# Six triangular inverses by two 16-step blocks and a join on TensorE, GpSimd's products moved to VectorE, softmax scalars to ScalarE

## The chip, the cores and the metric

One core of a Trainium2 chip. The metric is device time in microseconds, the median of several executions of one program. Engines are named as in the profile: PE (TensorE), DVE (VectorE), ACT (ScalarE), POOL (GpSimd), SP (SyncE, which only issues DMAs here).

## What is computed

A linear recurrence over 768 steps for 32 heads with 40x40 states, then two feed-forward blocks on its 3072 x 320 output (cut to what matters):

```
for t in range(S):
    y[t] = r[t] @ state
    Sa = state @ a[t]
    state = state * w[t] - outer(Sa, b[t]) + outer(v[t], k[t])
x = y                                    # 3072 x 320
h = x @ w_in                             # 320 -> 1024
solu = h * softmax(h)
x = ((solu - mean) / sqrt(var + 1e-6) * g) @ w_out
h = x @ w2_in                            # 320 -> 2048
out = (max(h, 0) + alpha * min(h, 0)) @ w2_out
```

The weights of both blocks arrive as 64-bit floats; the kernel rebuilds 32-bit values from their words ("decodes" them) and splits each into a high and a low part.

## The kernel before

**Stages.** The start (0 to 41 us) prepares windows 0 and 1. Then 24 slots (41 to 775 us): slot g takes 32 steps of the recurrence for all heads. In a slot PE runs, in this order, px (L654), pu (L669), pf (L694), pst (L708), pg (L747), pss (L728) and py (L772); each result passes through ACT or DVE before the next stage may use it. From slot 3 on the first feed-forward block is woven in as a queue of pieces (h L815, ptr L874, po L890 to L892, ptx L906), three slots behind. After the slots the second block runs nearly alone on PE (ph L1367, acc L1385 to L1387), with a short tail of the first.

**The order.** PE, DVE, ACT and POOL run the order in which the program is written out. `slot` writes it with a model of time: `now` is PE's clock in the plan, `run(e, cost, f, ...)` writes an instruction for engine e and advances e's planned time by a cost in microseconds. Work that is not urgent lies in the lists `work["dec"]`, `["inv"]`, `["scan"]`, `["xs"]`, from which `fill` takes the first that is ready. Where the plan has PE wait, and also where too few columns were streamed lately, `pop` writes a filler matmul ("busy" L315 in slots 0 to 3, "zero" L275 later); `flush(n)` writes the queued feed-forward pieces until n are left. SP's queue takes the DMAs in the order of writing.

**What the change touches.**
- The inverse of a 32x32 unit triangular matrix for every group of four slots (NT, read by pu and pf). `first_inverse` (group 0) splits it in two 16x16 blocks: 14 steps of a multiply and an add on DVE (L563, L566), a product with a mask (L571), a transpose (L573), and then two sets of small matmuls, pv and pn (L579). `inverse` (groups 1 to 5) does all 31 steps on DVE (L503, L507, L531) between two 128x1024 transposes (L515, L534).
- Each window (two slots) clamps the decay factors into a copy wc (L372), runs four scans over it (L376, L380) and multiplies kbf by the result on DVE (L430) and XS on POOL (L442).
- The masked pg of a slot: ACT copies PSUM to YS (L758), POOL multiplies by the mask (L752), py reads it.
- The low part of Y: POOL (L789). Then `x_move` writes Y to DRAM and reads it back transposed (L799 to L801).
- Softmax: four one-column operations on DVE (L822, L823, L834, L838).
- Decoding: four DVE operations per chunk (L932, L933, L940, L944), two on ACT, one product on POOL (L952); the raw words come by L969. `ND`, `NC`, `NL` say how many chunks of the second block's weights are due in each slot: the first four slots, the middle ones, the last four.

Of the kernel before, what the change touches and what calls it, by code (L numbers as in the profile page):

```python
# [45 lines left out]
def tile_kernel(ctx: ExitStack, tc: tile.TileContext, w_fm, a0_fm, a_fm, kb_fm, r_fm, v_fm, v_tm,  # L46
# [25 lines left out]
    half = flp.tile([128, 1], F32, name="half")  # L72
    xd = [dr.tile([640, 256], F32, name=f"xd{w}") for w in range(NW)]
# [62 lines left out]
    def init():  # L136
# [19 lines left out]
        nc.gpsimd.memset(half, -0.5)  # L156
        nc.gpsimd.memset(one, 1.0)
# [194 lines left out]
    def scan_steps(w, pe):  # L352
# [3 lines left out]
        def first():  # L356
# [47 lines left out]
    def prep_window(w):  # L404
# [32 lines left out]
    def mult_a(g, e, *pes):  # L437
# [4 lines left out]
        (nc.vector if w < 2 and e in DA else nc.gpsimd).tensor_tensor(out=o, in0=o, in1=h, op=ALU.mult)  # L442
# [5 lines left out]
    def gen1(g, half):  # L448
# [42 lines left out]
    def inverse(W):  # L491
        M, NT = LMN[2 * W % 3], LMN[(2 * W + 1) % 3]
        N = NT.rearrange("p s t -> p t s")

        P = PR[W > 0]

        def rank1(eng, tmp, s, rows):
            nt = 31 - s
            l = N[:, s + 1:32, s]
            tv = tmp[:, 0:sum(b - a for a, b in rows) * nt].rearrange("p (i t) -> p i t", t=nt)  # L500
            for a, b in rows:
                sh = [128, b - a, nt]
                eng.tensor_tensor(out=tv[:, a - rows[0][0]:b - rows[0][0]], in0=M[:, a:b, s:s + 1].to_broadcast(sh),  # L503
                                  in1=l.unsqueeze(1).to_broadcast(sh), op=ALU.mult)
            for a, b in rows:
                o = M[:, a:b, s + 1:32]
                r = eng.tensor_tensor(out=o, in0=o, in1=tv[:, a - rows[0][0]:b - rows[0][0]], op=ALU.add)  # L507
            return r

        def pool_rows():  # L510
            for s in range(P, 31):
                rank1(nc.gpsimd, b1.tile([128, TM], F32, name="tmp2", tag="Yt"), s, [(P, s + 1)])

        def start():
            nc.vector.transpose(out=N, in_=st["lraw", W].rearrange("p l t -> p t l"))  # L515
            run("P", 1.2, lambda: unit(M, nc.gpsimd), free["V"])
            pool_rows()

        def step(s):
            n, nt = min(s + 1, P), 31 - s  # L520
            m = n // 2
            if n <= SM:
                ops = [(M[:, i, s + 1:32], N[:, s + 1:32, s], M[:, i, s:s + 1]) for i in range(n)]
            elif nt <= SM:
                ops = [(M[:, 0:n, s + 1 + i], M[:, 0:n, s], N[:, s + 1 + i, s:s + 1]) for i in range(nt)]
            else:
                rank1(nc.vector, b1.tile([128, 256], F32, name="tmp"), s,
                                   [(0, m), (m, n)] if W == 0 else [(0, n)])
                return
            for o, x, f in ops:  # L530
# [1202 lines left out]
```

## Time and profile before

| what | us |
|---|---|
| median of 3 runs (1165.24 to 1170.81) | 1168.54 |
| the profiled execution | 1164.45 |
| its span | 1162.7 |
| start, 0 to 41.2 | 41.2 |
| slots 0 to 3, 41.2 to 197.2 | 156.0 |
| slots 4 to 19, 197.2 to 676.3 | 479.1 |
| slots 20 to 23, 676.3 to 774.7 | 98.4 |
| second block, 774.7 to 1162.7 | 388.0 |
| PE / DVE / ACT / POOL busy in the span | 1026.6 / 770.2 / 532.6 / 498.2 |

The bounds of a slot are the starts of its copy of px (XP, L657). [...]

### The profile page before, as it was taken

The numbers are of one execution on the slowest core, as the hardware profiler recorded it, in microseconds if no ns is written. First come the engines' busy times: TensorE is split into PE (matmuls) and PEld (weight loads), VectorE is DVE, ScalarE is ACT, GpSimd is POOL, SyncE is SP. The second block draws the span as 40 slices with busy tenths as digits, with TensorE's granted clock in tenths as the row PEclk, the third lists the DMA queues.
The fourth block names the chain that finished last, engine by engine and source line by source line (L and its number), as shares of the span: only waits on it lengthen the run. The fifth ranks groups of instructions, "written<-read, shape, count | busy, mean of one in ns | idle before, by whom it ended". The sixth has DMA issues, their size and how long they took to land. (4 is left out here: it accounts for less than half of the span.)

```text
span 1162.7 us, 38709 instructions
## 1 busy us (share of the span) xinstructions
PE 1026.6 (88%) x16801; PEld 818.1 (70%) x16801; DVE 770.2 (66%) x1471; ACT 532.6 (46%) x1218; POOL 498.2 (43%) x509
## 2 busy tenths in 40 slices
PE   6789686787868988888889989999899999999997
PEld 3455363676645766676657767779799999999996
DVE  8777898886869869778987974257434334443343
ACT  1355452564634754756447656658712121212121
POOL 6448556363325534553344323436233333333332
PEclk8789888888989989998999999999999999999999
DMA  5625542244332542443324532345502020201010
GB/s 167 156 72 136 139 136 70 71 125 107 97 102 81 134 131 59 129 128 105 81 57 124 155 83 62 79 130 185 174 1 66 4 65 4 66 4 45 1 24 14
DMA packets 106740, 103.70 MB, mean 89 GB/s; under 512 B 38340, under 2 KB 85188, under 8 KB 106564
## 3 DMA queue, kind: packets, MB, share of 16 engines
q1 hardware_dynamic: 106564, 101.17, 31.7%
q8 instruction: 133, 2.18, 0.8%
q14 instruction: 43, 0.35, 0.1%
HBM read 75.71 MB, written 25.43 MB: 87 GB/s over the span
## 5 line engine op out<-in xcount | busy, mean ns | idle before, releaser
L1374 POOL TENSOR_TENSOR gll<-gt,gh 128x512 fp32r<-128x512 f32 (+1 forms) x112 | 129.3, 1155 | 227.1 <-ACT gh L1373 224.4
L850 DVE TENSOR_SCALAR gt<-ph,al 128x512 f32<-128x512 f32 (+1 forms) x112 | 75.4, 674 | 189.0 <-PE ph L1367 188.9
L1373 ACT CAST gh<-gt 128x512 fp32r<-128x512 f32 (+1 forms) x112 | 62.6, 559 | 253.3 <-DVE gt L851 218.4
L752 POOL TENSOR_TENSOR YS<-YS,mask 64x512 f32<-64x512 f32 x48 | 64.9, 1353 | 105.3 <-ACT YS L758 103.4
L815 PE MATMUL h<-w1h,xt 128*128 128x512 f32 x240 | 91.2, 436 | 16.9 <-ACT h L836 16.9
L1386 PE MATMUL acc<-w2l,gh 128*128 128x320 f32 x288 | 89.0, 309 | 0.0
L1387 PE MATMUL acc<-w2h,gll 128*128 128x320 f32 x288 | 88.9, 309 | 0.0
L1385 PE MATMUL acc<-w2h,gh 128*128 128x320 f32 x288 | 88.9, 309 | 0.0
L890 PE MATMUL po<-wo1h,lnh 128*128 128x320 f32 x192 | 66.9, 348 | 21.6 <-DVE lnl L880 19.6
L442 POOL TENSOR_TENSOR XS<-XS,H 40x512 f32<-40x512 f32 (+1 forms) x48 | 70.0, 1461 | 35.2 <-DVE H L376 23.0
L952 POOL TENSOR_TENSOR dec<-em 128x256 f32<-128x256 f32 x44 | 38.0, 864 | 107.4 <-DVE em L944 58.9
L315 PE MATMUL busy<-busy 128*128 128x512 bf16 x292 | 80.1, 426 | 4.3 <-DVE busy L1281 3.0
L275 PE MATMUL zero<-D 104*128 104x512 bf16 x299 | 76.5, 393 | 1.5 <-DVE XS L482 1.5
L851 DVE SCALAR_TENSOR_TENSOR gt<-ph,gt 128x512 f32<-128x512 f32 (+1 forms) x112 | 68.8, 615 | 3.8
L507 DVE TENSOR_TENSOR LMN<-LMN,tmp 128x87 f32<-128x87 f32 (+8 forms) x135 | 67.7, 502 | 4.6
L503 DVE TENSOR_TENSOR tmp<-LMN,LMN 128x87 f32<-128x87 f32 (+8 forms) x135 | 67.6, 501 | 2.8
L892 PE MATMUL po<-wo1h,lnl 128*128 128x320 f32 x192 | 62.0, 323 | 4.4 <-DVE lnl L880 4.4
L815 PEld LDWEIGHTS h<-w1h,xt 128*128 128x128 f32 x240 | 44.7, 197 | 27.4 <-ACT h L836 20.6
L815 PE MATMUL h<-w1l,xt 128*128 128x512 f32 x144 | 62.7, 435 | 0.0
L622 ACT COPY KBS<-pt 64x160 f32<-64x160 f32 x192 | 55.1, 287 | 16.7 <-PE pt L618 14.4
L891 PE MATMUL po<-wo1l,lnh 128*128 128x320 f32 x192 | 61.7, 321 | 0.0
L1367 PE MATMUL ph<-w1h,w2h 128*128 128x512 f32 x180 | 59.4, 395 | 0.0
(209 smaller groups left out, 2705.6 us busy)
## 6 DMA issues: line engine op xcount, KB each, us to landing
kbf<-in_kb_fm_dram SPq DMA_DIRECT2D x24, 416.0 KB
x2d<-x SPq DMA_DIRECT2D x24, 320.0 KB
raw<-in_w_in_dram SPq DMA_DIRECT2D x24, 256.0 KB
xd<-Y SPq DMA_DIRECT2D x24, 256.0 KB
xt<-xd SPq DMA_DIRECT2D x12, 512.0 KB
raw<-in_w_out_dram SPq DMA_DIRECT2D x20, 256.0 KB
wt<-in_w_fm_dram SPq DMA_DIRECT2D x24, 211.7 KB
VUS<-in_v_tm_dram SPq DMA_DIRECT2D x48, 80.0 KB
```

Of the source, the lines that this page charges most:

```text
L275: nc.tensor.matmul(st["z"][0], lhsT=D1[:, 1:65].bitcast(BF16), rhs=D1[:, 0:256].bitcast(BF16), start=True, stop=True)
L315: nc.tensor.matmul(st["busy"], lhsT=busy[:, 0:128], rhs=busy, start=True, stop=True)
L442: (nc.vector if w < 2 and e in DA else nc.gpsimd).tensor_tensor(out=o, in0=o, in1=h, op=ALU.mult)
L503: eng.tensor_tensor(out=tv[:, a - rows[0][0]:b - rows[0][0]], in0=M[:, a:b, s:s + 1].to_broadcast(sh), in1=l.unsqueeze(1).to_broadcast(sh) ...
L507: r = eng.tensor_tensor(out=o, in0=o, in1=tv[:, a - rows[0][0]:b - rows[0][0]], op=ALU.add)
L815: nc.tensor.matmul(st["h"][:, ns], lhsT=l, rhs=r, start=j == 0, stop=j == len(ops) - 1)
L850: nc.vector.tensor_scalar(out=tmp, in0=h, scalar1=0.0, scalar2=al, op0=ALU.min, op1=ALU.mult)
L851: nc.vector.scalar_tensor_tensor(out=o, in0=h, scalar=0.0, in1=tmp, op0=ALU.max, op1=ALU.add)
L1374: nc.gpsimd.tensor_tensor(out=gll, in0=t, in1=f32(gh), op=ALU.subtract)
L1385: nc.tensor.matmul(acc, lhsT=gh[:, cs], rhs=oh, start=f == 0, stop=False)
L1386: nc.tensor.matmul(acc, lhsT=gh[:, cs], rhs=ol, start=False, stop=False)
L1387: nc.tensor.matmul(acc, lhsT=gll[:, cs], rhs=oh, start=False, stop=f == K2 - 1)
```

## The change

All six inverses use the two blocks and the join; GpSimd's products on XS, YS, Y and the first block's weights go to VectorE (the masked pg now straight from PSUM, so ACT's copy goes); the clamp of the decay factors goes, and the scans read wt; the softmax's small operations become three on ACT; the second block's decoding starts at slot 4; up to 10 feed-forward pieces stay queued before py (RES) and 8 at the end of a slot (KQ); and costs given as a tuple occupy, in the plan, a "port" that VectorE and GpSimd use one at a time.

```
-VS, NC, NL = 0, (2, 3, 1, 0), (3, 3, 3, 0)
-ND = (6, 6, 4, 2)
-RES = 2
-PR, SM, TM = (10, 32), 2, 121
+VS, NC, NL = 0, (2, 3, 3, 3), (3, 3, 3, 0)
+ND = (0, 0, 0, 0)
+KQ, RES = 8, 10
+YSV, XSV, YLV, DPV, VRV, W1V = 1, 1, 1, 0, 0, 1
...
         if not plain():
-            free[e] = max(free[e], *needs) + cost
+            t = max(free[e], *needs)
+            if isinstance(cost, tuple):
+                cost, = cost
+                for a, b in sorted(port):
+                    if a < t + cost and b > t:
+                        t = b
+                port.append((t, t + cost))
+                del port[:-6]
+            free[e] = t + cost
...
-            for s in ORDER[e]:
+            for s in ("dec",) * (st["slot"] % 4 < 3) + ORDER[e]:
...
-            nc.vector.tensor_scalar(out=wz[:, :, 1:65], in0=wv, scalar1=W_MAX, scalar2=W_MIN, op0=ALU.min, op1=ALU.max)
-            nc.vector.memset(wc[:, ::65], 0.0)
...
-        (nc.vector if w < 2 and e in DA else nc.gpsimd).tensor_tensor(out=o, in0=o, in1=h, op=ALU.mult)
+        (nc.vector if XSV or w < 2 and e in DA else nc.gpsimd).tensor_tensor(out=o, in0=o, in1=h, op=ALU.mult)
...
     def inverse(W):
-        M, NT = LMN[2 * W % 3], LMN[(2 * W + 1) % 3]
...
-    def first_inverse():
-        X, F = LMN[0], LMN[1]
+        X, F, A = LMN[(W + 1) % 2 if W else 0], LMN[(W + 1) % 2], LMN[2]
...
+        vec = [(2.2, start)] + [((0.38 + s * (15 - s) / 240.0,), lambda s=s: step(s)) for s in range(1, 15)] + [(2.0, fin)]
+        return vec, (0.75, low), [lambda: (left(0), left(1)), lambda: (join(0), join(1))]
...
+            for pe in range(2):
+                t = run("V", 0.43, lambda e=e, q=q, pe=pe: nc.vector.tensor_tensor(
+                    out=y[q, e, pe * 8:pe * 8 + 8], in0=pg[64 * pe:64 * pe + 64, :, e],
+                    in1=mask[64 * pe:64 * pe + 64].unsqueeze(1).to_broadcast([64, 8, 32]), op=ALU.mult), now[0] + PL)
...
-                        ("P", 1.3, lambda: nc.gpsimd.tensor_tensor(out=l, in0=Yt, in1=f32(h), op=ALU.subtract))], end)
+                        ("V" if YLV else "P", (0.7 if YLV else 1.3,), lambda: (nc.vector if YLV else nc.gpsimd).tensor_tensor(out=l, in0=Yt, in1=f32(h), op=ALU.subtract))], end)
...
         def small():
-            nc.vector.tensor_scalar(out=col(5), in0=col(1), scalar1=1e-9, scalar2=None, op0=ALU.add)
-            nc.vector.tensor_scalar(out=col(6), in0=col(5), scalar1=col(5), scalar2=1e-6, op0=ALU.mult, op1=ALU.mult)
+            nc.scalar.activation(out=col(6), in_=col(1), func=AF.Square, scale=1e-3, bias=tiny)
+            nc.scalar.activation(out=col(7), in_=col(4), func=AF.Identity, scale=1.0 / F1, bias=col(6))
...
-        for tasks in (turns, gens):
+        for tasks in (joins, turns, gens):
...
+            inverted(W + 1, p(2, 'z'), p(3, 'z'))
...
-        if g == 1:
+        if g == 2:
             until(lambda: decoded(6))
         stage_y(g)
         side(g, "z")
-        flush(0)
+        flush(0 if fin else KQ)
```

What moves on the engines, at three places. First PE in slot 8, the first that needs group 2's inverse (po is a feed-forward product, zero a filler, pu the first reader of the inverse, LMN). Before, 28 fillers stand directly in front of pu, 73 in the slot:

```order
L891 MATMUL po<-wo1l,lnh 128x320
L892 MATMUL po<-wo1h,lnl 128x320
L275 LDWEIGHTS D_148
L275 MATMUL zero<-D_148 128x512
...
L669 MATMUL pu<-XP,LMN_166 32x40 x12
```

and now:

```order
L593 MATMUL px<-VUS_168,XS_153 32x40 x32
L842 MATMUL po<-wo1h,lnh 128x320
L843 MATMUL po<-wo1l,lnh 128x320
L844 MATMUL po<-wo1h,lnl 128x320
...
L608 MATMUL pu<-XP,LMN_166 32x40 x32
L620 LDWEIGHTS D_149
L620 MATMUL pf<-D_149 32x256
L633 MATMUL pf<-LMN_166,XP 40x32 x16
```

No filler stands in slot 8 any more: three feed-forward pieces left over from the slot before stand in front of pu. Counted over the whole order by the same slot bounds, the fillers go from 232 to 174 in slots 0 to 3, from 239 to 127 in slots 4 to 19 and from 60 to 15 in slots 20 to 23.

Second, DVE in slot 9 up to the product that follows py (Yt). Before:

```order
L430 TENSOR_TENSOR kbf<-kbf,F 104x16x32
L713 TENSOR_TENSOR VUS_167<-pst,VUS_168 40x320 x4
L880 TENSOR_TENSOR lnl<-ptr,lnh 128x512 x2
L932 TENSOR_SCALAR em_5789<-raw_5739 128x256
...
L829 TENSOR_REDUCE sm<-h 128x1
...
L776 TENSOR_TENSOR Yt<-py,H 104x512
L834 TENSOR_SCALAR sm<-sm 128x1
```

and now:

```order
L443 TENSOR_TENSOR XS_153<-XS_153,H 40x512 x2
L443 TENSOR_TENSOR XS_154<-XS_154,H 40x512
L652 TENSOR_TENSOR VUS_168<-pst,VUS_169 40x320 x2
...
L431 TENSOR_TENSOR kbf<-kbf,F 104x16x32
...
L697 TENSOR_TENSOR YS_173<-pg_5872,mask 64x256 x4
L884 TENSOR_SCALAR em_5919<-raw_5863 128x256
...
L722 TENSOR_TENSOR Yt<-py,H 104x512
L785 TENSOR_REDUCE sm<-h 128x1
L736 TENSOR_TENSOR Y<-Yt,Y 104x16x32
```

XS, YS and Y's low part, which were POOL's, stand in DVE's row of work, and the one-column sm operation is gone.

Third, SP where window 4's Y moves through DRAM (xd and xt). Before:

```order
L799 DMA xd_72<-Y 32x8x256
L799 DMA xd_72<-Y 8x8x256
L800 DMA xt<-xd_72 128x4x256
...
L801 DMA xt<-xd_72 128x256
L349 DMA XS_154<-in_a_fm_dram 40x512
L969 DMA raw_6128<-in_w_out_dram 128x512
```

and now:

```order
L751 DMA xd_73<-Y 32x8x256
L751 DMA xd_73<-Y 8x8x256
L752 DMA xt<-xd_73 128x4x256
L923 DMA raw_6211<-in_w_in_dram 128x512
L753 DMA xt<-xd_73 128x256
```

The raw words of a decode chunk stand close behind xt, which waits for xd, in both.

## Rows read from the trace of the kernel before

**Rows 1.** Busy time by stage: us; PE, PEld, DVE, ACT, POOL; clock; DMA
```profile
197.20:676.30 479.10, 406.23 (x9412) 312.95 (x9412) 394.39 (x811) 276.91 (x673) 205.59 (x230) 0.92 0.39 105
774.70:1162.70 388.00, 375.11 (x2201) 342.42 (x2199) 164.83 (x263) 113.17 (x210) 139.44 (x121) 0.99 0.18 55
```
**Rows 2.** The same view of the fillers alone: "busy", then "zero" twice
```profile
41.20:197.20 156.00, 62.22 (x232) 21.87 (x232) 0.06 (x1) 0.00 (x0) 0.87 0.43 114
...
197.20:676.30 479.10, 59.24 (x228) 0.92 0.39 105
676.30:774.70 98.40, 13.16 (x53) 1.00 0.30 76
```
**Rows 3.** Groups of DVE in the slots, the five 31-step inverses
```profile
L507 DVE TENSOR_TENSOR LMN<-LMN,tmp 128x87 f32<-128x87 f32 (+8 forms) x135 | 67.7, 502 | 4.6
L503 DVE TENSOR_TENSOR tmp<-LMN,LMN 128x87 f32<-128x87 f32 (+8 forms) x135 | 67.6, 501 | 2.8
...
L515 DVE STREAM_TRANSPOSE LMN<-LMN 128x1024 f32<-128x1024 f32 x5 | 10.6, 2127 | 0.0
```
**Rows 4.** The same view of the one two-block inverse (group 0)
```profile
L566 DVE TENSOR_TENSOR LMN<-LMN,tmp 128x28 f32<-128x28 f32 (+6 forms) x14 | 3.4, 244 | 0.4
L563 DVE TENSOR_TENSOR tmp<-LMN 128x28 f32<-128x28 f32 (+6 forms) x14 | 3.4, 242 | 0.4
...
L573 DVE STREAM_TRANSPOSE VT<-V 128x512 f32<-128x512 f32 x1 | 1.1, 1093 | 0.0
```
**Rows 5.** Groups of PE in the slots: group 0's join, its two sets
```profile
L579 PE MATMUL pn<-VR,LMN 32*32 32x32 f32 x256 | 3.6, 213 | 2.3 <-issue 2.1 <-ACT LMN L589 0.2
L579 PE MATMUL pv<-VT,GR 16*32 16x16 f32 x256 | 2.7, 180 | 1.6 <-DVE VT L573 1.2 <-issue 0.4
```
**Rows 6.** Other groups of DVE in the slots
```profile
L482 DVE TENSOR_TENSOR XS<-pg,mask 32x256 f32<-32x256 f32 x80 | 33.2, 415 | 2.9 <-ACT LMN L473 1.9
...
L932 DVE TENSOR_SCALAR em<-raw 128x256 int32<-128x256 int32 x44 | 18.7, 426 | 37.9 <-DMA raw<-in_w_out_dram 20.8 <-DMA raw<-in_w_in_dram 13.5 <-POOL dec L952 3.3
...
L372 DVE TENSOR_SCALAR wc<-wt 104x512 f32<-104x512 f32 x19 | 12.2, 641 | 13.3 <-DMA wt<-in_w_fm_dram 13.2
...
L838 DVE TENSOR_SCALAR sm<-sm 128x1 f32<-128x1 f32 x21 | 4.4, 208 | 7.3 <-ACT h L836 6.5
```
**Rows 7.** Line L430 by itself: shortest/median/longest ns, first and last start
```profile
L430 DVE TENSOR_TENSOR kbf<-kbf,F x44: 674/690/1777, 12.0 to 625.1; 104x512 f32<-104x512 f32 x44
```
**Rows 8.** DVE in order of time (start, duration), slot 8
```profile
355.73 3.86 DVE L430 TENSOR_TENSOR kbf<-kbf,F 104x512 f32<-104x512 f32 x3
...
361.27 1.68 DVE L430 TENSOR_TENSOR kbf<-kbf,F 104x512 f32<-104x512 f32 x1
```
**Rows 9.** POOL in order of time, the same stretch
```profile
355.86 6.54 POOL L442 TENSOR_TENSOR XS<-XS,H 40x512 f32<-40x512 f32 x4
```
**Rows 10.** Groups of POOL in the slots
```profile
L752 POOL TENSOR_TENSOR YS<-YS,mask 64x512 f32<-64x512 f32 x48 | 64.9, 1353 | 105.3 <-ACT YS L758 103.4
L442 POOL TENSOR_TENSOR XS<-XS,H 40x512 f32<-40x512 f32 x40 | 59.6, 1489 | 25.9 <-DVE H L376 15.0 <-issue 7.8 <-DMA XS<-in_a_fm_dram 1.0
```
**Rows 11.** Who DVE waited for in slots 4 to 19: us, times, longest
```profile
DVE em L932 <- DMA raw<-in_w_out_dram: 20.1, 4, 9.4
DVE wc L372 <- DMA wt<-in_w_fm_dram: 13.2, 3, 7.0
```
**Rows 12.** Who PE waited for in the same stretch
```profile
PE po L890 <- DVE lnl L880: 19.0, 4, 9.6
PE h L815 <- ACT h L836: 14.3, 4, 12.7
```
**Rows 13.** SP in order of time, slot 8
```profile
329.57 0.39 SPq L800 DMA_DIRECT2D xt<-xd  x1
330.06 0.45 SPq L969 DMA_DIRECT2D raw<-in_w_out_dram  x1
```
**Rows 14.** DVE in order of time, slot 8
```profile
334.74 0.29 DVE L932 TENSOR_SCALAR em<-raw 128x256 int32<-128x256 int32 x1 [9.45 <-DMA raw<-in_w_out_dram]
```
**Rows 15.** Busy time by stage again: slots 9 and 10
```profile
379.00:402.40 23.40, 21.97 (x634) 17.22 (x632) 19.61 (x38) 18.09 (x47) 13.93 (x15) 1.00 0.52 144
402.40:432.90 30.50, 25.54 (x525) 20.47 (x526) 20.98 (x47) 15.70 (x39) 9.59 (x14) 0.83 0.43 116
```

More of the change, by code (lines that the diff above doesn't have):

```diff
@@ L491, in inverse @@
     def inverse(W):
-        M, NT = LMN[2 * W % 3], LMN[(2 * W + 1) % 3]
[L493 to L530, printed above, removed]
-                nc.vector.scalar_tensor_tensor(out=o, in0=x, scalar=f, in1=o, op0=ALU.mult, op1=ALU.add)
@@ L590, in left @@
                 ring[bk] = t + LAT
[L591 removed]
+                put(("left", W))(t + LAT)
         def join(h):
             ls = range(16 * h, 16 * h + 16)
[L595 removed]
+            until(("left", W))
             p, bk = bank([128, 16, 32], "pn")
@@ L599, in join @@
             ring[bk] = t + LAT
-            st["NT", 0] = F
-            put(("NT", 0))(t + LAT)
-        yield start
-        for s in range(1, 15):
-            yield lambda s=s: step(s)
-        yield fin
-        for f in (left, join):
-            for h in range(2):
-                yield lambda f=f, h=h: f(h)
+            st["NT", W] = F
+            put(("NT", W))(t + LAT)
+        vec = [(2.2, start)] + [((0.38 + s * (15 - s) / 240.0,), lambda s=s: step(s)) for s in range(1, 15)] + [(2.0, fin)]
+        return vec, (0.75, low), [lambda: (left(0), left(1)), lambda: (join(0), join(1))]
     def trans(w, q):
@@ L860, in soft @@
             return
-        chain(now[0] + PL, s[:5], lambda u: (put("h")(u), chain(
-            u, s[5:] + [("A", 1.27, lambda: norm(P, m))], put(("P", t)))))
+        chain(now[0] + PL, s[:4], lambda u: (put("h")(u), chain(
+            u, s[4:] + [("A", 1.27, lambda: norm(P, m))], put(("P", t)))))
     def tr1(t, j):
@@ L991, in rest, with zero @@
                 def rest():
-                    nc.gpsimd.tensor_tensor(out=w1l[:, k, cs], in0=o, in1=f32(w1h[:, k, cs]), op=ALU.subtract)
+                    (nc.vector if W1V else nc.gpsimd).tensor_tensor(out=w1l[:, k, cs], in0=o, in1=f32(w1h[:, k, cs]), op=ALU.subtract)
+                    if k == 2 and not W1V:
+                        zero()
+                def zero():
                     if k == 2:
@@ L997, in steps @@
                     ("A", 0.63, lambda: nc.scalar.copy(out=w1h[:, k, cs], in_=o)),
-                    ("P", 2.6 if k == 2 else 1.4, rest)]
+                    ("B", ("dec", (0.7,)), rest) if W1V else ("P", (2.6 if k == 2 else 1.4,), rest)] + [
+                        ("P", 1.2, zero)][:W1V * (k == 2)]
             return steps
@@ L1044, in ended @@
             q["done"] += 1
+            if q["wide"] and q["done"] == 6 and "moved" in st:
+                moved()
             if not q["wide"]:
@@ L1143, in slot_tasks, with inverted @@
             load_a(2 * u + 1)
-            lr = [("lr", h) for h in range(4 * W + 4, 4 * W + 8)]
-            inv = list(inverse(W + 1))
-            for i, (cost, f) in enumerate(inv):
-                work["inv"].append((lambda: max(map(at, lr)), cost, f,
-                                    put(("NT", W + 1)) if i == len(inv) - 1 else None))
+            inverted(W + 1, p(2, 'z'), p(3, 'z'))
         if c4 >= 2 and w < NW:
             load_a(2 * w + c4 - 2)
+    def inverted(W, first, last):
+        lr = [("lr", h) for h in range(4 * W, 4 * W + 4)]
+        vec, (cost, low), (lj, rj) = inverse(W)
+        for i, (c, f) in enumerate(vec):
+            work["inv"].append((lambda: max(map(at, lr)), c, f, None if i < len(vec) - 1 else
+                                lambda t: chain(t + LAT, [("A", cost, low)], lambda u: put(("VT", W))(u))))
+        joins.append((first, last, lambda: at(("VT", W)), lj))
+        joins.append((first, last, lambda: at(("left", W)), rj))
     def mlp_tasks(g):
@@ L1274, in phase1 @@
             kb_load(2)
-        inv = list(first_inverse())
-        st["joins"] = inv[16:]
-        for i, f in enumerate(inv[:16]):
+        vec, (_, low), st["joins"] = inverse(0)
+        for i, (_, f) in enumerate(vec):
             f()
```

104 lines of the change are left out of this document (46 added, 58 removed).

## The prediction

> **What bounds the kernel now.** I read the busy time by stage first. In the second block PE is busy 375.1 of 388.0 us [rows 1]; the change leaves that stage's instructions alone but for four softmaxes in its tail, so nothing is to be had there. The slots are another matter. In slots 4 to 19 DVE works 394.4 of 479.1 us and PE's own figure holds 59.2 us of "zero" fillers [rows 1, 2], which are written where the plan has PE wait or stream too little. [...]
>
> [...] (1) The inverse: groups 1 to 5 put 67.7 + 67.6 us of multiply and add and ten long transposes on DVE [rows 3], and slot 8 carries 73 fillers in front of and around its reader. (2) The exclusion between DVE and POOL: four kbf products in slot 8 take 3.86 + 1.68 us, though a product of that form alone takes 0.69 (the median; 0.67 the shortest, 1.78 the longest), and POOL's four XS products run in the very same stretch, 6.54 us [rows 7 to 9]. Each waits for the other. The masks that read PSUM show no such spread worth a term: their mean is 0.415 us [rows 6]. (3) A DMA: DVE stands 9.45 us in slot 8 until raw words land; their load was issued at 330.06, behind xt at 329.57, which had to wait for xd [rows 13, 14]. Such waits sum to 20.1 us for the one kind of raw words and 13.2 us for wt [rows 11], and PE's longest waits in this stretch, 19.0 us for lnl of DVE and 14.3 us for h of ACT [rows 12], are partly behind them.
>
> **The change part by part: slots 4 to 19.** On DVE, in us over the 16 slots:
> - Inverse. Five take 67.7 + 67.6 and two kinds of transposes at 10.6 each, so (156.5)/5 = 31.3 apiece [rows 3]. The two-block form takes 3.4 + 3.4, three transposes at 1.09 and one 128x512 product, for which I take kbf's 0.69: 10.8 [rows 4, 7]. Four of the five fall here: 4 x 20.5 = -82.
> - The clamp wc: 12.2/19 = 0.64 per half window, one per slot: -10 [rows 6].
> - Softmax: four one-column operations, of at most 0.21 each [rows 6], say 0.7 together: -11. They become three on ACT, which is busy 276.9 of 479.1 us [rows 1]; at 0.21 each that is 10 us, covered by its idle time. If it were not, the chain of a softmax would be that much later, 0.6 us per slot.
> - Masks from PSUM: four per slot at 0.415 (nearest row: the same kind of product, L482): +27. ACT loses its copies and POOL 64.9 us in all slots [rows 10].
> - XS: two per slot, two inputs in SBUF, 512 elements, like kbf: 0.69 (bounds 0.67 and 1.78): +22. Y's low part, the same form, +11.
> - Decoding: 18 chunks that ND placed in slots 0 to 3 now fall here, four operations of about 0.43 each [rows 6]: +31.
> - Exclusion: XS and YS leave POOL, two of its dearest readers (59.6 and 64.9 us [rows 10]). In slot 8 the four kbf products lost 5.54 - 4 x 0.69 = 2.8 us; eight windows at most 22, and none at least, since the median over all 44 did not wait. I take -16, with the smaller losses of the other forms.
>
> Sum: -28, so DVE's busy time goes from 394 to some 366 of these slots. What of that reaches the clock depends on DVE's idle 85 us. If all of it stays, the slots shrink by 28; if the shown DMA waits (33 us) vanish too, by 61. The order speaks against the second: the raw load stands close behind xt in the new program as well. For some of it speaks that 8 to 10 feed-forward pieces may now be carried past a slot's end, so PE has work when a late operand blocks it. From PE's side: 239 - 127 = 112 fillers at 59.24/228 = 0.26 are 29 us less, the two waits for lnl and h (33 us) perhaps halved, 17; against it four more joins at 3.6 + 2.7 = 6.3 us [rows 5], +25, and some clock won back. That gives -21 and a little more. I take the middle of DVE's two ends: **-45**, ends 0 and -80 (below).
>
> **Slots 0 to 3.** 232 fillers become 174: 58 x 62.22/232 [rows 2] = **-16**. What makes the room is 18 chunks fewer (31 us of DVE) and a shorter inverse against masks, XS, Y and 22 products of the first block's weights (22 x 0.69 = 15). One join more (6 us) stands in slot 3, where fillers stood. Ends 0 and -30: DVE is nearly always busy there, so a decode chunk in the wrong place costs its whole length.
>
> **Slots 20 to 23.** 60 fillers become 15; the trace has 53 in these bounds, 13.16 us, 0.25 each [rows 2]: 38 x 0.25 = **-9**. The last inverse, which slot 20 waited for, is the reason.
>
> **The rest.** The start loses five clamps of DVE, less than 0.7 us each, of which at most one is on the path to the first matmuls: 0 to -1, taken as 0. SP issues the same DMAs. In the tail, PE's 375 of 388 us cover the softmax [rows 1]; without that cover it would be 4 x 0.7.
>
> Sum: 1164.45 - 45 - 16 - 9 = 1094. The runs' median stands 4.1 us above this execution, well inside what I cannot know, so I leave **1094 us**. Differences within 0.5% (6 us) are what a measurement of this kernel can't tell from none.
>
> **The rivals.**
> (a) *Everything shown as a wait was made by the inverse and the exclusion, and goes.* Then slots 4 to 19 run like slot 9, 23.4 us, plus a quarter of a join, 1.6: 16 x 25 = 400, -79, and 1060 in all. For it: slot 9 had DVE at 19.6 of 23.4 us [rows 15], and the average after is 366/16 = 22.9. Against: the raw load still queued behind xt. 20%.
> (b) *The gain on DVE is eaten by PE's joins and by what is moved.* DVE's 28 us shrink the slots, 25 us of joins find no gap, and nothing else falls: slots 4 to 19 at about -3, 1136 in all. For it: work goes from POOL, busy 205.6 of 479.1 us, to the engine that is the fullest [rows 1]. [...] 14%.
> (c) *The clock falls with the fillers.* If every one of the 16 slots ran like slot 10 instead of six of them, 3.6 us more PE time each [rows 15], ten slots would lose 36 and the 45 would shrink to 9: 1130 to 1148. Against: the slots at the lower clock are those with DMA waits, not those without fillers; slot 9 has none in the order and runs at 1.00. [...] 5%.
> (d) *Slower: the masks queue.* DVE takes its work in order. YS, XS and Y now stand in a row with scans and kbf products; py waits for the mask, and if two long operations (1.7 us each, as the slow kbf [rows 8]) stand ahead of it at one point of each slot with no piece for PE, that is 3.4 x 24 = 82 us, and 1176. It decides from 70/24 = 2.9 us per slot. Against: in the new order the masks stand next to decode operations of 0.4 us, and PE has pieces in stock. 6%.
> (e) *No change*, several of these together: 3%.
>
> **How the numbers follow.** The forecast (1075 to 1115) has 52%, (a) 20%, (b) 14%, (c) 5%, (d) 6%, (e) 3%. The range 1047 to 1140 leaves out a part of (a) and of (b), half of (c), and (d) and (e), some 2 in 10. Faster by over 0.5%: forecast, (a), (b), (c), 91%; same 3%; slower 6%.
>
> **What would show it.** DVE's busy time in slots 4 to 19 near 366 us; kbf's products all near 0.69; two-block inverses at 10.8 us of DVE each; about 127 zero fillers and no long wait in slots 8 and 16; waits of DVE for raw words still there, 20 to 40 us; second block within 2 us of 388. The prediction is wrong if slots 4 to 19 take under 400 or over 460 us; then the row to look at is DVE's idle time, and who ended it.

## The result and the profile after

The changed kernel takes **1135.78 us** (median of 4 runs, 1133.65 to 1136.73) against 1166.89 us for the kernel before on the same chip: a ratio of 0.9734 (95% interval 0.969 to 0.9778), 31 us faster. The forecast was 1094 us, a gain of 70 on the execution it started from. The direction was right, the size less than half. The profiled execution took 1136.73 us, its span is 1134.9. By stage (bounds of a slot as before):

| stage | before, us | after, us | change | forecast |
|---|---|---|---|---|
| start | 41.2 | 41.0 | -0.2 | 0 |
| slots 0 to 3 | 156.0 | 140.0 | -16.0 | -16 |
| slots 4 to 19 | 479.1 | 478.6 | -0.5 | -45 |
| slots 20 to 23 | 98.4 | 83.8 | -14.6 | -9 |
| second block | 388.0 | 391.5 | +3.5 | 0 |

Nearly all that is missing is missing in slots 4 to 19. The busy time by stage, columns as in [rows 1]: stretch, its length, PE, PEld, DVE, ACT, POOL, clock, DMA share, GB/s:

```profile
41.00:181.00 140.00, 117.72 (x3307) 74.69 (x3308) 102.50 (x224) 57.58 (x135) 13.18 (x23) 0.84 0.37 101
181.00:659.60 478.60, 418.10 (x11342) 335.56 (x11340) 349.27 (x745) 279.67 (x688) 93.96 (x146) 0.89 0.42 113
659.60:743.40 83.80, 81.41 (x1881) 67.03 (x1881) 45.81 (x93) 59.58 (x140) 19.52 (x26) 0.98 0.35 93
743.40:1134.90 391.50, 378.52 (x2222) 347.86 (x2222) 164.40 (x254) 115.93 (x222) 140.37 (x123) 0.99 0.19 55
```

The same view of the filler "zero" alone (stretch, length, PE, clock, DMA share, GB/s):

```profile
181.00:659.60 478.60, 33.52 (x127) 0.89 0.42 113
```

Against [rows 1, 2], DVE's work in slots 4 to 19 fell from 394.39 to 349.27 us, even more than forecast, and its idle time grew from 85 to 129 us: the engine was relieved and the slots did not get shorter. PE tells why. Its busy time rose by 11.9 us although fillers fell by 25.7, so its other work rose by 37.6; its idle time fell by only 12.4. 37.6 - 25.7 - 12.4 = -0.5, the whole change of the stretch. Of the 37.6 us, 25.9 are the small matmuls of the four joins that now stand here (pv and pn, below); the rest is other work that took longer.

Who PE waited for in slots 4 to 19 (total, times, longest). "issue" stands where PE waited for nothing that the profile shows:

```profile
PE pn L523 <- issue: 10.6, 5, 4.1
PE pv L523 <- issue: 5.9, 4, 2.0
PE pg L686 <- ACT VUF L636: 4.9, 1, 4.9
...
PE pu L608 <- issue: 2.8, 1, 2.8
PE po L843 <- issue: 2.5, 1, 2.5
PE pss L667 <- issue: 2.5, 2, 2.2
```

The long waits of [rows 12] for lnl and h are gone (the longest for h is 1.3 us). In their place "issue" takes 29.7 us in nine rows; before, two rows of pg had 1.0 us each. pv and pn are the two sets of small matmuls of a join. Their groups in all slots:

```profile
L523 PE MATMUL pn<-VR,LMN 32*32 32x32 f32 x1536 | 19.2, 205 | 13.5 <-issue 13.3 <-ACT LMN L533 0.2
L523 PE MATMUL pv<-VT,GR 16*32 16x16 f32 x1536 | 19.1, 192 | 11.1 <-issue 10.4 <-DVE VT L515 0.7
```

These are six joins with 38.3 us of work, 6.4 each where 6.3 was read from [rows 5], and 23.7 us of gaps to which the view gives no cause. The idle column of [rows 5] already had 2.1 + 0.4 us of "issue" for the one join before. PE in order of time in slot 11 (start, duration, ..., idle before):

```profile
407.09 1.59 PE L523 MATMUL pv<-VT,GR 16*32 16x16 f32 x168
...
410.85 0.83 PE L523 MATMUL pv<-VT,GR 16*32 16x16 f32 x77 [0.43 <-issue]
...
413.57 0.54 PE L523 MATMUL pn<-VR,LMN 32*32 32x32 f32 x39
414.87 1.30 PE L523 MATMUL pn<-VR,LMN 32*32 32x32 f32 x128 [0.77 <-issue]
420.26 1.43 PE L523 MATMUL pn<-VR,LMN 32*32 32x32 f32 x89 [4.09 <-issue]
```

The joins stand in the last slot of each group, and these are now the long ones: slots 7, 11, 15 and 19, which took 27.1, 24.9, 22.7 and 20.2 us before. Now, with clocks (third column from the end) of 0.71 to 0.89:

```profile
267.90:299.70 31.80, 27.86 (x1018) 22.34 (x1017) 19.85 (x44) 16.88 (x41) 7.29 (x10) 0.89 0.30 78
388.90:426.40 37.50, 30.84 (x1040) 24.47 (x1038) 23.04 (x57) 19.15 (x49) 6.83 (x11) 0.88 0.37 97
501.90:538.40 36.50, 33.23 (x1016) 26.78 (x1016) 18.68 (x49) 15.54 (x39) 8.21 (x10) 0.71 0.26 68
622.00:659.60 37.60, 32.40 (x1024) 26.16 (x1023) 21.84 (x58) 18.16 (x43) 6.08 (x10) 0.77 0.40 112
```

### The profile page after: what moved, and what is told of

Read it like the earlier page. It is cut to its first block, busy times and chain, and to the rows that moved or that the text cites. A ratio compares the mean times of both kernels' runs of the same rounds, so it can differ in the third digit from the quotient of the medians.

```text
span 1134.9 us, 43057 instructions
## 1 busy us (share of the span) xinstructions
PE 1022.4 (90%) x19146; PEld 839.8 (74%) x19146; DVE 697.2 (61%) x1372; ACT 524.6 (46%) x1214; POOL 290.6 (26%) x358
## 3 DMA queue, kind: packets, MB, share of 16 engines
q8 instruction: 152, 2.49, 0.9%
## 4 chain that ended last, share of the span: by engine, by line
PE 67%; DVE 14%; DMA 8%; issue 6%; ACT 4%; POOL 1%; SPq 0%; DVEq 0%; ACTq 0%; POOLq 0%
PE ph L1330 15%; PE h L767 7%; PE acc L1350 5%; PE acc L1349 5%; PE acc L1348 5%; PE busy L325 3%; PE pf L633 2%; DMA raw<-in_w_in_dram 2%; PE py L718 2%; PE pss L667 2%; DMA raw<-in_w_out_dram 2%; PE zero L285 2%; PE po L842 2%; PE pst L647 2%; DMA xd<-Y 2%
## 5 line engine op out<-in xcount | busy, mean ns | idle before, releaser
L767 PE MATMUL h<-w1h,xt 128*128 128x512 f32 x240 | 97.6, 466 | 1.4 <-ACT h L775 1.3
L325 PE MATMUL busy<-busy 128*128 128x512 bf16 x234 | 70.2, 454 | 5.1 <-DVE busy L1243 3.8
L767 PE MATMUL h<-w1l,xt 128*128 128x512 f32 x144 | 67.8, 471 | 0.0
L652 DVE TENSOR_TENSOR VUS<-pst,VUS 40x320 f32<-40x320 f32 x92 | 45.0, 489 | 32.9 <-PE pst L647 30.8
L577 POOL MEMSET YS<- 64x512 f32 x44 | 22.9, 521 | 141.3 <-PE py L718 140.1
L671 ACT COPY KBS<-pss 40x320 f32<-40x320 f32 x92 | 38.6, 420 | 38.1 <-PE pss L667 36.9
L767 PEld LDWEIGHTS h<-w1h,xt 128*128 128x128 f32 x240 | 47.9, 213 | 10.4 <-ACT h L775 2.1
L1348 PEld LDWEIGHTS acc<-w2h,gh 128*128 128x128 f32 x288 | 54.1, 188 | 1.2
L1349 PEld LDWEIGHTS acc<-w2l,gh 128*128 128x128 f32 x288 | 54.1, 188 | 1.2
```

The costliest lines, as they stand in the source:

```text
L325: nc.tensor.matmul(st["busy"], lhsT=busy[:, 0:128], rhs=busy, start=True, stop=True)
L767: nc.tensor.matmul(st["h"][:, ns], lhsT=l, rhs=r, start=j == 0, stop=j == len(ops) - 1)
L1348: nc.tensor.matmul(acc, lhsT=gh[:, cs], rhs=oh, start=f == 0, stop=False)
L1349: nc.tensor.matmul(acc, lhsT=gh[:, cs], rhs=ol, start=False, stop=False)
```

## The experiments

Three theories. **J**: the joins stand on PE's path and cost far more than their own 6.4 us. **C**: the clock fell because there are fewer fillers. **V**: VectorE and its transfers still end the slots, and the rest is shifted waiting. All kernels start from the changed one, and each was timed beside the kernel before on its chip; differences are therefore taken between ratios and multiplied by 1166.9 us. The intervals of the ratios are about 0.4% to either side, so a difference of under some 7 us between two runs can't be told from none. Three of the kernels (without the joins, the same PE time in few instructions, each in one pass) put zeros where the joins' results belong and so compute no inverse; they are there for their times.

### Without the joins

```
 def units(p, lhsT, rhs, rows, ls):
+    if W:
+        nc.tensor.matmul(p.rearrange("p l c -> p (l c)"), lhsT=D1[:, 1:65].bitcast(BF16), rhs=D1[...].bitcast(BF16), ...)
...
     for l in ls:
-        for q in range(0, 128, 32):
+        for q in range(0, 0 if W else 128, 32):
```

> Leaves out the joins of groups 1 to 5: the 2 x 128 small matmuls of each become three 128x512 matmuls that write zeros, in the same order of all other work. Theory J (the joins stand on PE's path with their own 6.4 us each, 3.3 to 5.5 us of gaps without a wait before them, and a lower clock behind them): five joins x 11 = 55 us less, up to 75 with the clock: 1060 to 1081 us, and the long slots 7, 11, 15, 19 come down from 32 to 38 us to under 28. Theory C (fewer fillers, so a lower clock in every slot): the clock of slots 4 to 19 stays at 0.89 and at most 15 us go: 1120 or more. Theory V (VectorE and its DMA waits still end the slots): under 10 us, waits of PE for DVE and ACT take the place: 1126 or more.

Measured: 1069.47 us, ratio 0.9184 (0.9137 to 0.9232), 64 us under the changed kernel, 12.8 per join. (In place of each join stand four zero matmuls, two of 256 and two of 512 columns, 5.3 us in all.) The four join slots, with their sum:

```profile
250.50:272.20 21.70, 20.82 (x510) 15.58 (x509) 19.71 (x44) 16.74 (x41) 7.27 (x10) 1.00 0.40 108
357.30:382.60 25.30, 25.16 (x537) 19.20 (x536) 22.25 (x56) 18.66 (x49) 6.04 (x10) 1.00 0.40 96
458.30:479.20 20.90, 19.28 (x500) 14.27 (x500) 18.44 (x48) 15.13 (x38) 8.24 (x10) 1.00 0.40 104
565.40:589.50 24.10, 23.50 (x528) 18.19 (x527) 20.41 (x55) 17.71 (x42) 6.09 (x10) 1.00 0.44 121
sum 92.00, PE 88.75 PEld 67.24 DVE 80.81 ACT 68.24 POOL 27.65; mean PE 22.19 PEld 16.81 DVE 20.20 ACT 17.06 POOL 6.91
```

All are at clock 1.00 and take 92 us in place of 143. The sums of the changed kernel's four join slots, first whole, then its small matmuls alone (L523):

```profile
sum 143.40, PE 124.33 PEld 99.75 DVE 83.41 ACT 69.73 POOL 28.40; mean PE 31.08 PEld 24.94 DVE 20.85 ACT 17.43 POOL 7.10
sum 143.40, PE 25.94; mean PE 6.48
```

So the 51.4 us that the four joins cost in their own slots have three parts. The small matmuls are 25.9 us where the stand-in zeros are 4.2: 21.8 more. PE's idle time is 19.1 us where it is 3.2: 15.8 more. The rest of PE's work, nearly the same instructions, takes 98.4 us where it takes 84.6: 13.8 more, at clocks of 0.71 to 0.89 where it is 1.00. Per join this is some 5.4, 4.0 and 3.5 us.

Slots 4 to 19 of the run without joins as one row:

```profile
162.80:589.50 426.70, 384.42 (x9320) 305.50 (x9319) 346.62 (x742) 278.12 (x687) 93.63 (x146) 0.93 0.45 124
```

That is 52 us less than with the joins, at the same DVE work and with as many fillers (125 for 127). C and V fall for the changed kernel, J holds at its price.

### Every small matmul of a join twice

```
-        for q in range(0, 128, 32):
+        for q in (*range(0, 128, 32),) * (2 if W else 1):
```

> Each small matmul of the joins of groups 1 to 5 is issued twice, the plan is the same. Theory J: each join costs its own 6.4 us again and some gaps: +32 to +60 us, 1168 to 1196. Theory C: +0 to +10. Theory V: the joins lie beside DVE's work, +0 to +10, 1136 to 1146.

Measured: 1214.5 us, ratio 1.0451 (1.0413 to 1.0488): +84 us, 16.7 per doubled join, above the range that J gave. PE in the third doubled join (group 3's, in order of time) shows how:

```profile
456.20 1.30 PE L523 MATMUL pn<-VR,LMN 32*32 32x32 f32 x128 [2.27 <-issue]
459.67 1.93 PE L523 MATMUL pn<-VR,LMN 32*32 32x32 f32 x128 [2.17 <-issue]
463.14 1.43 PE L523 MATMUL pn<-VR,LMN 32*32 32x32 f32 x89 [1.54 <-issue]
```

Work and gap alternate in portions of 128 matmul records (the last portion is 89 records of pn and, behind them, 38 of px); weight loads are as many as matmuls, 128 beside the 128 matmuls that start at 414.87 us in the changed kernel. Here there is one portion per 3.47 us, of which 1.3 to 1.9 are work; the portions of pv in the same join start 3.8 and 4.0 us apart (434.40, 438.21 and 442.23 us). Two DMA queues are of the kind "instruction". The packets of one of them, q8 (packets, MB, share), keep step with PE's records (PE and PEld): 133 for 33602 before the change, one per 252.6, and 152 for 38292 after it, one per 251.9. After the change:

```profile
q8 instruction: 152, 2.49, 0.9%
```

Without the joins:

```profile
q8 instruction: 132, 2.16, 0.8%
```

With the joins doubled:

```profile
q8 instruction: 172, 2.82, 1.0%
```

Twenty packets for five joins either way: 2.49 MB in 152 packets is 16 KB each, so a join is 64 KB of instructions in four packets, and four portions of 3.5 to 4.0 us are 14 to 16 us, near the 16.7 that doubling a join costs. That packets and gaps belong together can be seen in time. In the stretch from 452 to 466 us, in 40 slices of 0.35 us, little else moves after the first slices, and three single packets stand out (47 GB/s):

```profile
GB/s 146 140 357 322 313 255 98 277 202 18 30 6 0 0 0 47 0 0 0 0 0 0 0 0 0 47 0 0 0 0 0 0 0 0 0 47 0 0 0 0
```

By the trace's packet times, those of q8 start here at 453.56, 457.30, 460.78 and 464.27 us, and the first three are followed by the portions at 456.20, 459.67 and 463.14, 2.4 to 2.6 us after their packet's start; the next packet starts 1.1 us after a portion does. In the changed kernel 16 of the 17 "issue" gaps of slots 4 to 19, 28.6 of their 29.8 us, end 2.3 to 2.7 us after the start of a packet of q8, the last one 3.0 us after. That the joins, and the other steps that have "issue" in the table of PE's waits, wait for their own code there is my reading of these times; no view names what PE waits for.

### The same PE time in few instructions

```
+            if W:
+                for i in range(10 if p.shape[2] == 32 else 10):
+                    nc.tensor.matmul(...the zero matmul of the run without joins...)
             for l in ls:
-                for q in range(0, 128, 32):
+                for q in range(0, 0 if W else 128, 32):
```

> As the kernel without joins, but in place of each join of groups 1 to 5 PE gets about the same time in few instructions: 20 zero matmuls of 256 columns and 20 of 512, some 6.5 us. The join's price was 66.3 / 5 = 13.3 us (1135.8 against 1069.5). If it is PE time and nothing else that counts, and every us of it costs about two because later steps wait, this run is back near 1136 (1125 or more). If 6.5 us of it are PE's own time and the rest is the supply of instructions and the clock behind tiny matmuls, the price here is at most 6.5 us: 1069.5 + 32 = 1102 or less, with hardly an unexplained gap and a clock over 0.93 in slots 4 to 19.

Measured: 1093.86 us, ratio 0.9387 (0.9351 to 0.9423): 24 us over the run without joins, 4.7 per join. The zeros are 34.6 us of PE work in all (5.3 us in the run without joins). The join slots have no gap left; the first two of the four:

```profile
255.60:282.00 26.40, 26.40 (x546) 19.21 (x545) 19.68 (x43) 17.04 (x42) 7.29 (x10) 1.00 0.34 86
370.10:400.20 30.10, 30.10 (x570) 22.29 (x570) 22.96 (x57) 19.11 (x49) 6.82 (x11) 1.00 0.42 111
```

This is the second reading of the expectation: about as much PE time as a join's own costs some 4.7 of the 12.8 us; 8 belong to something that comes with many small instructions.

### The same number of matmuls, each in one pass

```
-  lhsT=lhsT[q:q + rows, l, 0:32], rhs=rhs[q:q + rows, l, :],
+  lhsT=ident[q:q + rows, z:z + 16].bitcast(BF16) if W else ..., rhs=ident[q:q + rows, z:z + n // 2].bitcast(BF16) if W else ...,
```

The operands are bfloat16 zeros, cut out of the identity.

> The joins of groups 1 to 5 keep their 256 matmuls in the program, but on bfloat16 zeros, which need one pass where 32-bit floats need two (the output is zeros): 256 matmul and 256 weight-load records per join for 512 and 512. If the price goes with the instructions, 13.3 us becomes 6 to 7: 1100 to 1105, and PE's instruction packets fall from 152 by 10. If the fetched bytes alone make the gaps and a first stretch is held in advance, more than half of the price goes: 1085 to 1100. If the gaps are not from supply, the gaps before pv and pn stay at 20 us or more and only the own time halves: 1115 or more.

Measured: 1090.06 us, ratio 0.9363 (0.9322 to 0.9404): 4.2 us per join over none. The packets are 142, ten fewer as expected. Half the instructions (640 records in each of the two sets of the five joins, where 32-bit floats have 1280) cost a third of the price, 4.2 of 12.8 us, as the second reading of the expectation has it. In the doubled join above 188 records of pv ran before the first gap, but that a first stretch is held in advance was not tested by itself.

### Supply or clock: zeros in front of the full joins

```
+    for i in range(10 if W else 0):
+        nc.tensor.matmul(...the zero matmul..., start=True, stop=True)
     for l in ls:
         for q in range(0, 128, 32):
```

> The joins of groups 1 to 5 stay as after the change, and in front of each quarter of a join PE also gets the ten zero matmuls of the run with few instructions: 34 us more of PE work in all, which alone cost 24 us there (1093.9 against 1069.5). If the rest of a join's price is the supply of instructions (one packet of 16 KB per 3.5 us, as the doubled joins show, with 1.3 to 1.6 us of matmuls each), the zeros run while PE would wait for packets: 0 to 10 us more than 1136, the gaps before pv and pn under 12 us instead of 22. If it is the clock behind small matmuls, the zeros cost and give back: the gaps stay and the clock of slots 7, 11, 15 and 19 rises to over 0.9. If neither, the costs add: 1155 or more.

Measured: 1147.69 us, ratio 0.9862 (0.981 to 0.9914): +15 us, between the bounds, and by the time alone undecided: 15 against the 24 us that the zeros cost without joins is a difference inside the intervals. The groups of the small matmuls say more:

```profile
L526 PE MATMUL pv<-VT,GR 16*32 16x16 f32 x1536 | 17.6, 183 | 7.9 <-issue 6.1 <-DVE VT L515 1.8
L526 PE MATMUL pn<-VR,LMN 32*32 32x32 f32 x1536 | 17.1, 198 | 2.2 <-issue 2.1 <-ACT LMN L536 0.2
```

The "issue" gaps fall from 23.7 to 8.2 us, under the 12 that the expectation gives for supply. What the clock does is seen in the join slots:

```profile
261.60:296.90 35.30, 33.46 (x1059) 24.68 (x1058) 19.89 (x44) 16.93 (x42) 7.33 (x10) 0.95 0.27 71
382.30:422.30 40.00, 36.56 (x1080) 27.22 (x1079) 23.05 (x57) 19.16 (x48) 6.82 (x11) 0.96 0.36 98
502.70:537.00 34.30, 32.60 (x1055) 24.44 (x1055) 18.55 (x48) 15.36 (x38) 8.18 (x10) 0.97 0.28 71
622.00:663.30 41.30, 36.48 (x1064) 26.55 (x1064) 21.83 (x58) 18.10 (x43) 6.07 (x10) 0.92 0.40 112
sum 150.90, PE 139.11 PEld 102.89 DVE 83.32 ACT 69.55 POOL 28.41; mean PE 34.78 PEld 25.72 DVE 20.83 ACT 17.39 POOL 7.10
```

The clock is up from between 0.71 and 0.89 to between 0.92 and 0.97. The four slots together are not shorter (151 us for 143), but they hold 30.5 us of zeros (L522) more. So 23 us came back in them: 7 of idle time, 4 of the small matmuls (25.9 to 22.2 us) and 12 of the other work of PE (98.4 to 86.4 us). Neither of the two explanations is enough alone: the gaps did what was expected for supply, and the other work of these slots took 98.4 us at clocks of 0.71 to 0.89, 86.4 at 0.92 to 0.97 and 84.6 at 1.00 (without joins), which is the 3.5 us per join above. What stays open: whether the lower clock goes with the gaps or with the small matmuls themselves, since the changed kernel has both in the same slots.

### Two ways to hide the supply

One waiting feed-forward piece behind every 16 small matmuls:

```
+                if W and l % 4 == 3 and head():
+                    pop()
```

> In the joins of groups 1 to 5 one waiting feed-forward piece is put behind every 16 small matmuls, if one is ready. If the gaps before pv and pn (23.7 us in all) come from PE's supply of instructions, which 128 small matmuls with 128 weight loads in a row exhaust, they fall under 10 us and the time by 10 to 25: 1111 to 1126. If they come from something else (the clock, DVE), they stay and the time moves by under 6 us.

Measured: 1132.36 us, ratio 0.9731 (0.9697 to 0.9765): no difference from the changed kernel that can be told. The "issue" gaps before pv and pn fell to about half (between 150 and 700 us from 22.1 to 11.2 us), the 10 to 25 us that were expected of it did not come. Perhaps the pieces spent here are missing later; that was not followed. And the plan told of a join's true cost:

```
-                pace(0.042, 16)
+                pace(0.1 if W else 0.042, 16)
```

> The plan is told that four small matmuls of a join take 0.1 us (as measured: 6.4 us for 64 such fours) and not 0.042, so it puts feed-forward pieces between them and moves what follows. Theory J: as the spread join, 5 to 25 us less, 1111 to 1131. Theory V: the plan's error of 3.7 us per join is taken up by waits anyway: within 6 us.

Measured: 1127.89 us, ratio 0.9705 (0.9679 to 0.9731). 3 us by the ratios, 8 by the medians, and the intervals overlap: inconclusive, at the low end of J's range or under it.

### The other parts of the change, undone one by one

Products back on GpSimd:

```
-YSV, XSV, YLV, DPV, VRV, W1V = 1, 1, 1, 0, 0, 1
+YSV, XSV, YLV, DPV, VRV, W1V = 0, 0, 0, 0, 0, 0
```

> The products on YS, XS, Y and the first block's weights go back to GpSimd (the masked pg by ScalarE's copy first), with the plan's port rule kept; all else as after the change. Theory J (PE's chain bounds the slots, VectorE has 129 us to spare): VectorE's busy time in slots 4 to 19 falls by about 60 us, some long kbf products come back, the time stays within 12 us of 1136. [...]

Measured: 1148.71 us, ratio 0.9849 (0.9802 to 0.9896), +13 us, clear of the noise: just outside J's band. DVE had 312.90 us in slots 4 to 19, 36 less, not 60, and the exclusion was back (shortest, median, longest ns):

```profile
L431 DVE TENSOR_TENSOR kbf<-kbf,F x44: 672/684/1776, 12.0 to 597.8; 104x512 f32<-104x512 f32 x44
```

The old stock of feed-forward pieces:

```
-KQ, RES = 8, 10
+KQ, RES = 0, 2
```

> After the change, but 2 feed-forward pieces are kept before py and none at a slot's end, as before the change. Theory J: the joins stand at a slot's end, where then no piece is left for PE to do while it waits for the copies of pv and pn: 2 to 4 us more in each join slot and some in the others, 1146 to 1166. If the kept pieces are worth nothing: within 6 us of 1136.

Measured: 1153.31 us, ratio 0.9909 (0.9877 to 0.9941), +20 us as J said. The old places of the decoding:

```
-VS, NC, NL = 0, (2, 3, 3, 3), (3, 3, 3, 0)
-ND = (0, 0, 0, 0)
+VS, NC, NL = 0, (2, 3, 1, 0), (3, 3, 3, 0)
+ND = (6, 6, 4, 2)
```

> After the change, but with the second block's decoding due as before it (18 chunks in slots 0 to 3). I said that moving them takes 31 us from VectorE in slots 0 to 3 and gives 31 to slots 4 to 19. If VectorE is not the bound in slots 4 to 19, as the 129 us of idle time say, the move cost nothing there and is worth its 16 to 31 us in slots 0 to 3: 1150 to 1170. If it only shifts the load: within 8 us of 1136.

Measured: 1140.37 us, ratio 0.9791 (0.976 to 0.9823), +7 us with intervals that overlap, a miss of the first expectation and inside the second: where the decoding stands hardly matters.

Now the inverse alone (the three edits above together, so only the two-block inverse, the softmax scalars, the missing clamp and the port rule stay):

> Of the change only the inverse in two blocks, the softmax scalars, the missing clamp and the port rule: products on GpSimd, feed-forward queue (2 and 0 pieces kept) and decoding due as before the change. Theory J: five joins give back 66 us of what VectorE's 102 us bring, so the inverse alone is worth little: 1140 to 1165 us, and the rest of the change makes the difference to 1136. Theory V: the inverse alone brings 25 us or more: 1138 or less.

Measured: 1199.45 us, ratio 1.0311 (1.0263 to 1.0359): **slower** than the kernel before by 3%, worse than either theory said. Why was not followed in its trace; undone one by one the three edits cost 13, 20 and 7 us, together 67. And the rest of the change alone:

```
-            inverted(W + 1, p(2, 'z'), p(3, 'z'))
...
+            inv = list(old_inverse(W + 1))
+            for i, (cost, f) in enumerate(inv):
+                work["inv"].append((lambda: max(map(at, lr)), (cost,), f, ...))
```

> Groups 1 to 5 use the 31-step inverse of the kernel before again, on VectorE, with no join; everything else of the change stays. Theory J: PE loses the joins (as in the kernel without them, 1069.5), VectorE gets 20.5 us back per group, in slots 4 to 19 some 349 + 82 = 431 us of 427, so it becomes the bound there with at least the 40 us it has to wait for transfers and for PE: 1105 to 1135, a little less than the change. Theory V (VectorE's load was the limit all along and the two blocks are what helps): 1150 or more.

Measured: 1194.01 us, ratio 1.0247 (1.0208 to 1.0287), also slower than before. I expected 1105 to 1135 by J; what came is V's side, 1150 or more: with the long inverses VectorE is a bound. Slots 12 and 16, the first readers of a new inverse:

```profile
418.20:491.30 73.10, 57.37 (x785) 37.17 (x786) 54.99 (x119) 26.68 (x64) 11.20 (x17) 0.86 0.30 83
561.20:624.00 62.80, 52.24 (x756) 34.18 (x757) 47.30 (x103) 26.24 (x63) 9.99 (x16) 0.86 0.31 86
```

and the fillers in them:

```profile
418.20:491.30 73.10, 27.73 (x109) 0.86 0.30 83
561.20:624.00 62.80, 23.79 (x86) 0.86 0.31 86
```

What took 28.5 and 26.1 us in the changed kernel became 73.1 and 62.8, with 27.7 and 23.8 us of fillers: DVE, now with the products too, has a 31-step inverse ready so late that the plan fills PE with zeros until pu may read it. Each half of the change loses alone and both together win 2.7%: the products need the short inverse, and the joins, as the old stock's 20 us suggest, need the pieces.

### A version that beats both

Half the instructions with real data: the join's operands are rounded to bfloat16, a change of the computation in its last digits, so each small product is one pass (768 records in each set of the six joins, where the changed kernel has 1536).

```
-    VR = ca.tile([128, 32, 32], F32, name="VR")
+    VR = ca.tile([128, 32, 32], BF16, name="VR")
...
+    VB = ca.tile([128, 32, 16], BF16, name="VB")
...
+        def block():
+            nc.scalar.copy(out=GB[:, :, 16:32], in_=GR[:, :, 16:32])
+        def thin():
+            nc.scalar.copy(out=VB, in_=VT)
```

> The joins of all groups take their operands rounded to bfloat16 (three tiles, two more ScalarE copies of 128x512 per group), so each small product is one pass and not two; nothing is left out but these digits. Theory J: as with the one-pass joins on zeros (1090), the two copies stand beside other work: 1086 to 1104, PE's instruction packets 140 to 142. Theory V: within 10 us of 1136.

Measured: 1095.36 us, ratio 0.9437 (0.9392 to 0.9481), 140 packets, as J said. It stands beside the one-pass joins on zeros (0.9363, overlapping intervals), so those were not fast because of their zeros. With the plan's cost of four small matmuls at 0.06 us (`pace(0.06, 16)`):

> The bfloat16 joins (operands rounded), and the plan takes 0.06 us for four small matmuls and not 0.042. The same step brought 8 us with 32-bit joins. Theory J (what is left of a join, some 4 us, is PE time and hardly a wait): within 8 us of 1095.

Measured: **1082.63 us**, ratio 0.9306 (0.9266 to 0.9346), 12 us under the 1095 that was expected to within 8, and the best of all that keep the result: by the ratios 81 us under the kernel before, 50 under the changed one. Slots 4 to 19:

```profile
162.90:601.00 438.10, 388.37 (x10310) 310.02 (x10309) 349.83 (x755) 286.00 (x703) 98.38 (x150) 0.94 0.46 123
```

The forecast had 434 us for this stretch: with cheap joins it comes out close to that.

## Why the prediction was right and wrong

- **What bounds the kernel** was right for before and not carried through. DVE's load, the exclusion and the inverse did hold the slots; the run with the old inverse shows how hard the inverse still would.
- **The DVE sum** held to a few us term by term, but for one term. The inverse takes 7.1 us of multiply and add, 3.3 of transposes and 0.7 for the product with the mask per group, 11.1 where 10.8 was forecast:

```profile
L509 DVE TENSOR_TENSOR LMN<-LMN,tmp 128x28 f32<-128x28 f32 (+6 forms) x56 | 14.2, 254 | 1.9
L506 DVE TENSOR_TENSOR tmp<-LMN 128x28 f32<-128x28 f32 (+6 forms) x56 | 14.1, 252 | 1.3
...
L499 DVE STREAM_TRANSPOSE LMN<-GR 128x512 f32<-128x512 f32 x4 | 4.5, 1137 | 0.1
...
L513 DVE TENSOR_TENSOR LMN<-LMN,tri 128x512 f32<-128x512 f32 x4 | 2.8, 693 | 0.1
```

  The term that failed is the decoding. It was put at +31 us for 18 chunks moved into slots 4 to 19; there were 32 operations of each of its four lines in them before and 40 after, and the four lines together went from 54.5 to 58.0 us, +3.4. This is the main reason why DVE ended at 349 and not 366 us.

- **The exclusion** held: kbf's longest product is 1229 ns, where [rows 7] had 1777, its median 684; in these slots the 32 products went from 34.5 to 22.2 us, 12 of the 16 us that were taken.

```profile
L431 DVE TENSOR_TENSOR kbf<-kbf,F x44: 675/684/1229, 13.0 to 594.8; 104x512 f32<-104x512 f32 x44
```

- **The step that failed** is the choice in slots 4 to 19: "I take the middle of DVE's two ends: -45". That number holds for a kernel in which PE has nothing new to do: without joins the stretch fell by 52.4 us, inside DVE's ends of 28 and 61. The joins stood only in the sum from PE's side (+25, which gave -21) and were dropped with it. They had to be added to DVE's middle, since the slots passed from DVE to PE. And the term itself was half of what it is: 4 x 6.3 = 25 us forecast, 52 measured (478.6 - 426.7), since the sum priced a join by the busy column of [rows 5] alone. The 2.5 us of "issue" in the idle column beside it would have made it 4 x 8.8 = 35. What the join slots showed is 25.9 us of the joins' own work, as forecast, 15.8 us of idle time and 13.8 us by which the slots' other work became slower at the lower clock, less 4.2 us for the stand-in zeros.
- **Slots 0 to 3** came out at -16.0 by luck: the fillers fell by 58 as forecast, but their time only from 62.2 to 53.2 us, and without the join the slots fall by another 20.6 us (140.0 to 119.4). The join that I put "where fillers stood" at no cost was not covered; the rest brought more than I said.
- **Slots 20 to 23** gave 14.6 for 9, and the second block lost 3.5 where nothing was forecast; neither was followed further.
- **Waits**: DVE's waits for raw words stayed, 34.7 us (forecast 20 to 40), and the fillers are 127 as in the order. PE's long waits for lnl and h went altogether, more than the half that I took; 29.7 us of "issue" came in their place.

```profile
DVE em L884 <- DMA raw<-in_w_out_dram: 20.2, 8, 8.8
...
DVE em L884 <- DMA raw<-in_w_in_dram: 14.5, 7, 5.3
```

- **"Some clock won back"** was wrong: 0.92 became 0.89. It was not the fillers, so rival (c) falls: with as many of them and no join it is 0.93.
- **Rival (b)**, 1136 us at 14%, is what happened, by one of its two mechanisms: PE's joins ate the gain, what was moved to DVE did not. That its figure fits is partly luck: it set 28 us of gain against 25 of joins, and the runs show 52 against 52. With the products back on GpSimd the kernel is 13 us slower, and kbf's longest product is 1776 ns again.
- The range ended at 1140 and held the time only by its margin for (b); that the kernel gets faster, given 91%, was right.

## What to carry to other kernels

When a change relieves the engine that bounds a stretch and loads another, add the other's new work to the shortened stretch; don't hide it beside an engine that is no longer the bound. Price small matmuls by their instructions: 256 products of 32-bit floats were 64 KB of code here and cost twice their busy time (12.8 us for 6.4). Fewer passes paid (1095 us for 1136); other work between or in front of the products made the gaps smaller (11.2 us for 22.1, and 8.2 for 23.7) and the kernel not measurably faster (1132 and 1148 us). And read the idle column of the nearest row, "issue" above all, before taking its busy time as the price.

## What the runs showed of the hardware

In the doubled join whose times stand above, a dense run of small matmuls with their weight loads went on in portions of 128 matmul records. The pn portions start 3.47 us apart with 1.3 to 1.9 us of work in each, those of pv 3.8 and 4.0, and each of the three portions of pn started 2.4 to 2.6 us after a 16 KB packet of the instruction queue q8. Nothing in the views marks the gap but "issue"; in slots 4 to 19 of the changed kernel 16 of 17 such gaps ended 2.3 to 2.7 us after a packet's start. That PE waits for instructions in them is an inference from these times. A 32-bit product has two records (256 for a set of 128 matmuls), a bfloat16 one has one (128); with zeros for operands that took ten packets (142 for 152) and two thirds of the price (4.2 us per join for 12.8) away.

Gaps of this kind stood beside a low granted clock: 0.71 to 0.89 in the join slots with them, 0.96 to 1.00 in those with about the same PE time in few instructions, which have no gap. With zeros in front of the joins the clock was 0.92 to 0.97, and the other work of the four join slots took 86.4 us where it had taken 98.4, 12 us less; the zeros took 30.5.
